# Two tokens a partition for V, tiles of 32 keys, and a first weight slice cast by two engines

## The chip, the cores and the metric

The kernel runs on one core of a Trainium2 chip. Five engines work side by side on it: TensorE (PE in the profile; PEld is its weight load), VectorE (DVE), ScalarE (ACT), GpSimd (POOL) and SyncE (SP), which here issues nearly all transfers (SPq in the profile). The metric is the time of one execution on the device, in microseconds (us); less is better. The kernel before takes 278.19 us, the median of three runs (277.95 to 278.23).

## The reference: what is computed

Attention inside chunks of 64 tokens (8 batches, 8 heads, 576 tokens, 64 numbers a head), and behind it a two-layer network with a squared ReLU on all 4608 tokens:

```
scores = scale * matmul(q_c, k_c^T)          # in chunks of 64 tokens
attn   = exp(scores - max) / (sum + 1e-9)
x      = matmul(attn, v_c)                    # [4608, 512], heads side by side
h      = max(x @ w_in, 0)                     # w_in  [512, 2048]
out    = (h * h) @ w_out                      # w_out [2048, 512]
```

Inputs and output are float32. The kernel multiplies in bfloat16 and leaves the maximum out of the exponential, which does not change the quotient.

## The kernel before, in words

The tokens are cut into 18 groups of 256, and two groups make a block of 512 tokens, so there are nine blocks. For each block the network's first layer runs 16 feature tiles of 128 (`ffn_in`, L621 for its matmuls), the second runs after it (`ffn_out_by_ft` for block 0, L795; `ffn_out` for the others, L678). The attention of the next blocks is set by hand into slots between these matmuls (L392, L420 and others), and the loads for later blocks go out on SP in between. The order within each engine is the program's own: nothing is rearranged by a planner, and an instruction that waits holds back all behind it on its engine.

The change lies in the start, where the attention of block 0 has no earlier work to hide behind. It is done by heads, not by tokens: half 0 is heads 0 to 3 of the block's 512 tokens, half 1 is heads 4 to 7. In the order of the program:

- `load_half` (L235) loads Q and K of each half, 512 KB each, with four tokens a partition, in pieces of 1024 bytes. SP issues Q0, K0, Q1, K1 (L238).
- `load_v_half` (L244) loads V, for each half in four transfers of 128 KB, one for each 128 tokens; a partition holds one token, so pieces have 256 bytes (L247). V goes into memory that the array `w_sum` needs only later, with a column of ones beside each head (memset at L231), so that the values product gives the sum of the exponentials too.
- `load_w_in(0, n_cast=2)` (L837): SP issues the first of eight slices of w_in, 512 KB for 256 features (L173), into one of five staging buffers `w_st`; POOL casts it to bfloat16 in two pieces of 128 features (L176).
- `transpose_half` (L255) transposes Q and K on PE and copies the result out of PSUM (L277, DVE and ACT). `scores_half` (L279) makes the scores of a half, keys on the partitions, as 32 matmuls of 64 keys by 64 queries (L289), and ACT takes the exponential (L296).
- `values_half` (L301) multiplies for half u and tokens 256j to 256j + 255: 16 matmuls of 64 by 65 (L309), a reciprocal (L316) and a product (L317) on DVE. `transpose_x_half` (L323) turns the result for the network (L325 on PE, copied by ACT or DVE at L329).
- `keep_busy(n)` (L333) issues n matmuls on constants, whose result nobody reads (L337).

Scores and values use two PSUM buffers in turn (`ps_att`), the rest four (`ps_ffn`). Two feature tiles of the network are begun (`begun`) before `ffn_in` takes over: they use the half of the input that comes from heads 0 to 3 first.

After the start SP issues the other seven slices of w_in and eight of w_out (L181), each cast on POOL, and with them Q, K and V of group 2, then of group 3 (L110, L158, L162). A staging buffer is free for slice i + 5 when the cast of slice i is done.

Of the kernel before, what the change touches and what calls it, by code (L numbers as in the profile page):

```python
# [10 lines left out]
FP32 = mybir.dt.float32  # L11
BF16 = mybir.dt.bfloat16
AF = mybir.ActivationFunctionType
ALU = mybir.AluOpType
# [3 lines left out]
def kernel(  # L18
# [9 lines left out]
    nc = tc.nc  # L28

    B, H, S, D = q.shape  # L30
# [4 lines left out]
    n_hp = H // 2  # L35
# [131 lines left out]
        for f in pieces:  # L167
            f()

    def load_w_in(i, n_cast=1):  # L170
        cols = slice(i * 256, (i + 1) * 256)
        st = wst_pool.tile([128, 1024], FP32, name="w_st").rearrange("p (a f) -> p a f", a=n_dt)
        nc.sync.dma_start(out=st, in_=moe_w_in[:, cols].rearrange("(a p) f -> p a f", p=128))  # L173
        n = 256 // n_cast
        for c in range(0, 256, n):
            nc.gpsimd.tensor_copy(  # L176
                out=w_in_bf[:, :, i * 256 + c:i * 256 + c + n], in_=st[:, :, c:c + n])
# [34 lines left out]
    def transpose_qk(g, q_pool, k_pool):  # L212
# [13 lines left out]
            transpose_paired(g, which, bank)  # L226
            copy_paired(copy, qkT[:, which], bank)

    v_first = w_sum.rearrange("p i f c -> p (i f c)")[:, 0:8 * H * (D + 1)].bitcast(
        FP32).rearrange("p (t h d) -> p t h d", t=4, h=H)  # L230
    nc.gpsimd.memset(v_first[:, :, :, D:D + 1], 1.0)  # L231

    first = chunks[blocks[0][0]][0]
# [9 lines left out]

    def load_v_half(u):  # L244
        b, s = first
        for t in range(4):
            nc.sync.dma_start(  # L247
                out=v_first[:, t, 4 * u:4 * u + 4, 0:D],
                in_=v[b, 4 * u:4 * u + 4, s + 128 * t:s + 128 * t + 128, :].rearrange(
                    "h s d -> s h d"))  # L250

# [27 lines left out]
    def scores_half(qkT):  # L279
# [3 lines left out]
        for h in range(2):  # L283
# [17 lines left out]
    def values_half(e, x, u, j):  # L301
        v_bf = v_first.bitcast(BF16)
        ps = ps_att.tile([128, 2, 512], FP32, name="ps_att")
        for t in range(2):
            for h in range(2):
                for a in range(2):
                    for p in range(2):
                        o0 = (2 * t + h) * (D + 1)
                        nc.tensor.matmul(  # L309
                            out=ps[64 * p:64 * p + 64, a, o0:o0 + D + 1],  # L310
                            lhsT=e[64 * p:64 * p + 64, a, h, 2 * j + t, :],
                            rhs=v_bf[64 * p:64 * p + 64, 2 * j + t, 4 * u + 2 * h + a, 1::2],
                            start=True, stop=True)
        o = ps[:, :, 0:4 * (D + 1)].rearrange("p a (h d) -> p a h d", d=D + 1)
        rec = att_pool.tile([128, 2, n_hp], FP32, name="rec", bufs=4)
# [688 lines left out]
```

## Time and profile before

| | |
|---|---|
| median of three runs | 278.19 us (277.95 to 278.23) |
| profiled execution, its time | 277.18 us |
| its span in the trace | 275.4 us |
| granted TensorE clock | 1.00 |
| PE busy | 267.3 us, 97% |
| first matmul of the network (L621) | 17.89 us |
| first matmul of block 0's second layer (L795) | 32.02 us |
| transposes of K of group 3 (L201) | 49.20 us |

All times inside an execution come from the one profiled execution and count from the start of its span. The time of that execution is 1.8 us longer than its span, and 1.0 us shorter than the median of the runs without a profile. A row of the timeline gives start, busy time, engine, line, operation, what is written and what is read, and in brackets how long the engine had been idle and what ended it. In the windows each row is a stretch of time, followed by the busy time of PE, PEld, DVE, ACT and POOL with their counts, the granted clock, the mean busy share of the 16 DMA engines and the rate in GB/s.

### The profile page before, as it was taken

The page shows a single profiled execution, that of the slowest core. Times are in us where ns is not written, and L with a number is a line of the kernel's source. Part 1 is how long each engine was busy: PE and PEld are TensorE (multiplying, and loading weights), DVE is VectorE, ACT ScalarE, POOL GpSimd, SP SyncE. Part 2 cuts the span into 40 slices and gives each one's busy share as a digit, 9 for nine tenths or more (in the row PEclk, how much of TensorE's full clock was granted, in tenths as well). Part 3 has the DMA queues.
Part 4 walks back from the last instruction along what each step waited for, and adds up shares of the span by engine and source line. Part 5 has one row for each costly group of instructions (what it writes and reads, how often), then busy time and mean ns, then how long its engine had stood idle before and what let it go on. Part 6 is the DMA issues. An engine that isn't in the chain of part 4 may idle for free.

```text
span 275.4 us, 7355 instructions
## 1 busy us (share of the span) xinstructions
PE 267.3 (97%) x3047; PEld 185.5 (67%) x3047; DVE 202.2 (73%) x313; ACT 155.5 (56%) x262; POOL 92.9 (34%) x106
## 2 busy tenths in 40 slices
PE   7889999999999999999999999999999999999994
PEld 4544454888775587658755875587658755875683
DVE  1546516689986997599769776977599769777793
ACT  1537605796347782768186918682768186317710
POOL 2037768140433800380029002900380029003412
PEclk9999999999999999999999999999999999999999
DMA  7999999999999999999999799858799981623004
GB/s 233 228 334 356 369 340 233 227 224 181 286 167 189 261 199 176 292 236 185 259 249 210 153 187 286 189 115 181 225 280 181 210 317 38 193 47 108 0 2 152
DMA packets 136417, 57.11 MB, mean 207 GB/s; under 512 B 110336, under 2 KB 130048, under 8 KB 136384
## 3 DMA queue, kind: packets, MB, share of 16 engines
q1 hardware_dynamic: 135968, 55.72, 86.8%
q0 software_dynamic: 272, 0.79, 0.7%
q8 instruction: 24, 0.39, 0.6%
q10 hardware_dynamic: 144, 0.13, 0.1%
q14 instruction: 9, 0.07, 0.1%
HBM read 36.70 MB, written 9.44 MB: 168 GB/s over the span
## 4 chain that ended last, share of the span: by engine, by line
PE 81%; DMA 9%; SPq 7%; POOL 1%; issue 1%; DVE 0%
PE ps_ffn L678 36%; PE ps_ffn L621 32%; PE ps_ffn L508 8%; DMA w_st<-in_moe_w_in_dram 5%; SPq L247 3%; PE ps_att L420 2%; DMA k_sb<-in_k_dram 2%; DMA w_st<-in_moe_w_out_dram 2%; PE ps_att L392 2%; SPq L162 1%; POOL w_in_bf L176 1%; SPq L158 1%; SPq L238 1%; PE ps_att L447 1%; SPq L181 0%
## 5 line engine op out<-in xcount | busy, mean ns | idle before, releaser
L621 PE MATMUL ps_ffn<-xT,w_in_bf 128*128 128x512 bf16 (+1 forms) x528 | 111.2, 353 | 0.4 <-POOL w_in_bf L176 0.4
L634 POOL TENSOR_TENSOR gT<-rl 128x512 bf16<-128x512 f32 x40 | 45.9, 1162 | 121.1 <-ACT rl L585 120.2
L621 PEld LDWEIGHTS <-w_in_bf 128*128 128x128 bf16 x528 | 50.6, 98 | 37.2 <-POOL w_in_bf L176 1.8
L678 PEld LDWEIGHTS <-w_st 128*128 128x128 bf16 x640 | 62.2, 98 | 7.3
L585 ACT ACTIVATE rl<-ps_ffn 128x512 f32<-128x512 f32 x84 | 50.1, 597 | 29.3 <-PE ps_ffn L621 29.0
L634 DVE TENSOR_TENSOR w_st<-gT 128x2048 bf16<-128x2048 bf16 x40 | 47.4, 1219 | 6.0 <-ACT gT L588 5.9
L678 PE MATMUL ps_ffn<-w_out_bf,w_st 128*128 128x256 bf16 x384 | 45.1, 273 | 0.0
L634 DVE TENSOR_TENSOR gT<-rl 128x512 bf16<-128x512 f32 x30 | 20.8, 693 | 22.6 <-ACT rl L585 22.2
L678 PE MATMUL ps_ffn<-w_sum,w_st 128*128 128x256 bf16 x256 | 29.6, 273 | 0.0
L678 PEld LDWEIGHTS <-gT 128*128 128x128 bf16 x256 | 24.7, 98 | 5.1 <-ACT gT L588 0.6
L612 ACT ACTIVATE rl<-ps_ffn 128x256 bf16<-128x256 f32 (+1 forms) x48 | 20.4, 455 | 6.6 <-PE ps_ffn L621 5.6
L525 DVE SCALAR_TENSOR_TENSOR gT<-rl 128x512 bf16<-128x512 f32 x21 | 23.2, 1103 | 0.4
L616 DVE TENSOR_TENSOR gT<-rl 128x256 bf16<-128x256 bf16 (+1 forms) x41 | 16.2, 438 | 9.6 <-ACT rl L612 9.5
L785 ACT COPY o_sb<-ps_ffn 128x512 f32<-128x512 f32 x7 | 4.1, 587 | 33.6 <-PE ps_ffn L678 33.6
L428 DVE TENSOR_TENSOR x<-ps_att,rec 128x512 bf16<-128x512 f32 x32 | 22.1, 692 | 1.1
L403 ACT ACTIVATE e<-ps_att 128x1024 bf16<-128x1024 f32 x16 | 15.8, 1025 | 4.8 <-PE ps_att L392 4.8
L508 PEld LDWEIGHTS <-w_dif 128*128 128x128 bf16 x140 | 12.9, 98 | 7.1
L678 PE MATMUL ps_ffn<-w_out_bf,gT 128*128 128x256 bf16 x128 | 15.6, 273 | 0.0
L678 PE MATMUL ps_ffn<-w_sum,gT 128*128 128x256 bf16 x128 | 15.3, 273 | 0.0
L176 POOL CAST w_in_bf<-w_st 128x1024 bf16<-128x1024 f32 (+1 forms) x9 | 8.9, 1000 | 17.9 <-DMA w_st<-in_moe_w_in_dram 17.9
L795 PE MATMUL ps_ffn<-w_out_bf,gT 128*128 128x512 bf16 x64 | 14.5, 380 | 0.0
L588 ACT ACTIVATE gT<-rl 128x512 bf16<-128x512 f32 x21 | 13.3, 632 | 0.7
(81 smaller groups left out, 288.8 us busy)
## 6 DMA issues: line engine op xcount, KB each, us to landing
q_sb<-in_q_dram SPq DMA_DIRECT2D x16, 512.0 KB, 6.2
out_dram<-o_sb SPq DMA_DIRECT2D x14, 512.0 KB, 4.6
k_sb<-in_k_dram SPq DMA_DIRECT2D x24, 256.0 KB, 5.9
w_st<-in_moe_w_in_dram SPq DMA_DIRECT2D x8, 512.0 KB, 6.7
w_st<-in_moe_w_out_dram SPq DMA_DIRECT2D x8, 512.0 KB, 6.1
ve_sb<-in_v_dram SPq DMA_DIRECT2D x28, 128.0 KB, 3.7
vo_sb<-in_v_dram SPq DMA_DIRECT2D x21, 128.0 KB, 3.3
k_sb<-in_k_dram SPq DMA_DIRECT2D x4, 512.0 KB, 6.8
```

Source lines behind the costliest of these rows:

```text
L403: nc.scalar.activation(out=e_out, in_=s_in, func=AF.Exp, scale=scale)
L428: nc.vector.tensor_tensor(out=x[:, t].rearrange("p h a d -> p a h d"), in0=o[:, :, :, 0:D], in1=rec.to_broadcast([128, 2, n_hp, D]), op=AL ...
L508: nc.tensor.matmul(out=out[:, 256 * f:256 * f + 256], lhsT=a[:, d, 128 * f:128 * f + 128], rhs=b[:, :, d, :], start=(first and f == 0 and ...
L525: later.append(lambda: nc.vector.scalar_tensor_tensor(out=place_of(i, jj), in0=both(x), scalar=0.0, in1=both(x), op0=ALU.max, op1=ALU.mult))
L585: nc.scalar.activation(out=rl, in_=h, func=AF.Relu)
L588: nc.scalar.activation(out=gT[:, ft], in_=rl, func=AF.Square)
L612: nc.scalar.activation(out=rl[:, 0:n], in_=h[:, 0:n], func=AF.Relu)
L616: nc.vector.tensor_tensor(out=gT[:, ft, c:c + n], in0=rl[:, 0:n], in1=rl[:, 0:n], op=ALU.mult)
L621: nc.tensor.matmul(out=h[:, 0:n], lhsT=w_in_bf[:, dt, ft * 128:(ft + 1) * 128], rhs=xT[:, c // 128:(c + n) // 128, dt, :], start=(dt == 0) ...
L634: engine.tensor_tensor(out=out, in0=in0, in1=in1, op=op)
L678: nc.tensor.matmul(out=outs[t], lhsT=a[:, i, t * 128:(t + 1) * 128], rhs=b[:, i, :], start=(first and i == 0 and (last or t == 0)), stop=( ...
L795: nc.tensor.matmul(out=o_ps[tt], lhsT=gT[:, ft, tt * 128:(tt + 1) * 128], rhs=w_out_bf[:, ft, :], start=(ft == 0), stop=(ft == n_ft - 1))
```

## The change

V of heads 0 to 3 is laid out anew: a partition holds two neighbouring tokens, so two transfers of 256 KB in pieces of 512 bytes take the place of four of 128 KB in pieces of 256 bytes. V of heads 4 to 7 stays as it was. Since the 64 keys of a chunk then lie on 32 partitions, even and odd keys apart, the scores of half 0 are made in tiles of 32 keys (64 matmuls instead of 32) and the values as two products of 32 keys that add up in PSUM (32 matmuls instead of 16). The column of ones stands ahead of the even token and behind the odd one, so that the two sums land in different columns; a reduction on DVE adds them before the reciprocal.

The first w_in slice is loaded at the same place in SP's order, but its cast is taken out of `load_w_in` and put behind the last transposes, as four pieces of 2 x 128 features by 128: POOL casts those of feature tile 0, ACT those of feature tile 1. Slices 1 to 3 are cast in two pieces each, no longer in one. In the order of PE, `values_half(e1, 1)` moves ahead of the transposes of x(1,0), and the two `keep_busy` calls of 4 and 6 become 2 and 3.

```diff
-    def load_w_in(i, n_cast=1):
+    def load_w_in(i, n_cast=1, cast=True):
...
+        if not cast:
+            return st
...
+    VE = 2 * D + 2
+    HH = H // 2
+    v_first = w_sum.rearrange("p i f c -> p (i f c)").bitcast(FP32)
+    v_pairs = v_first[:, 0:2 * HH * VE].rearrange("p (t h e) -> p t h e", t=2, h=HH)
...
+    nc.gpsimd.memset(v_pairs[:, :, :, 0::VE - 1], 1.0)
...
     def load_v_half(u):
         b, s = first
+        if u == 0:
+            for t in range(2):
+                nc.sync.dma_start(
+                    out=v_pairs[:, t, :, 1:1 + 2 * D],
+                    in_=v[b, 0:4, s + 256 * t:s + 256 * t + 256, :].rearrange(
+                        "h (s i) d -> s h (i d)", i=2))
+            return
...
+    def scores_pairs(ps, qT, kT):
+        for h in range(2):
+            for t in range(2):
+                for i in range(2):
+                    for c in range(4):
+                        for a in range(2):
+                            rows = slice(64 * a, 64 * a + 64)
+                            o0 = a * 512 + h * 256 + t * 128 + i * 64
+                            nc.tensor.matmul(
+                                out=ps[32 * c:32 * c + 32, o0:o0 + 64],
+                                lhsT=kT[rows, h, 4 * t + c, i::2],
+                                rhs=qT[rows, h, 4 * t + c],
+                                start=True, stop=True, tile_position=(64 * a, 32 * c))
+
+    def values_pairs(e, x, j):
...
+        for h in range(2):
+            for a in range(2):
+                for i in range(2):
+                    for c in range(4):
+                        t, p = divmod(c, 2)
+                        rows = slice(32 * c, 32 * c + 32)
+                        o0 = (2 * h + a) * (D + 2) + i
+                        nc.tensor.matmul(
+                            out=ps[64 * p:64 * p + 64, t, o0:o0 + n],
+                            lhsT=e[rows, a, h, 2 * j + i, :],
+                            rhs=v_bf[rows, j, 2 * h + a, 1::2][:, i * n:i * n + n],
+                            start=(h == a == i == 0), stop=(i == 1),
+                            skip_group_check=True, tile_position=(32 * c, 64 * p))
...
+        nc.vector.tensor_reduce(
+            out=rec, in_=o[:, :, :, 0::D + 1], op=ALU.add, axis=mybir.AxisListType.X)
+        nc.vector.reciprocal(out=rec, in_=rec)
+        nc.vector.tensor_tensor(
...
-    load_w_in(0, n_cast=2)
+    w_first = load_w_in(0, cast=False)
...
-    e0 = scores_half(qkTs[0])
+    e0 = scores_half(qkTs[0], pairs=True)
...
-    values_half(e0, xs[0], 0, 0)
+    values_pairs(e0, xs[0], 0)
     keep_busy(2)
     e1 = scores_half(qkTs[1])
-    values_half(e0, xs[0], 0, 1)
+    values_pairs(e0, xs[0], 1)
     transpose_x_half(xs[0], 0, 0, A, bank_bf16())
-    keep_busy(4)
-    values_half(e1, xs[1], 1, 0)
+    keep_busy(2)
+    values_half(e1, xs[1], 0)
     transpose_x_half(xs[0], 0, 1, A, bank_bf16())
-    keep_busy(6)
+    values_half(e1, xs[1], 1)
+    keep_busy(3)
     xb = [bank_bf16(), bank_bf16()]
     begun = {ft: ps_ffn.tile([128, 512], FP32, name="ps_ffn") for ft in range(2)}
     transpose_x_half(xs[1], 1, 0, A, xb[0])
-    values_half(e1, xs[1], 1, 1)
     keep_busy(3, begun[0])
     transpose_x_half(xs[1], 1, 1, V, xb[1])
+    for dt in (slice(0, 2), slice(2, 4)):
+        for ft, copy in enumerate((nc.gpsimd.tensor_copy, nc.scalar.copy)):
+            cols = slice(128 * ft, 128 * ft + 128)
+            copy(out=w_in_bf[:, dt, cols], in_=w_first[:, dt, cols])
...
     for i in range(1, 8):
-        load_w_in(i)
+        load_w_in(i, n_cast=2 if i < 4 else 1)
```

More of the change, by code (lines that the diff above doesn't have):

```diff
@@ L227, in transpose_qk @@
             copy_paired(copy, qkT[:, which], bank)
-    v_first = w_sum.rearrange("p i f c -> p (i f c)")[:, 0:8 * H * (D + 1)].bitcast(
-        FP32).rearrange("p (t h d) -> p t h d", t=4, h=H)
+    VE = 2 * D + 2
+    HH = H // 2
+    v_first = w_sum.rearrange("p i f c -> p (i f c)").bitcast(FP32)
+    v_pairs = v_first[:, 0:2 * HH * VE].rearrange("p (t h e) -> p t h e", t=2, h=HH)
+    v_first = v_first[:, 2 * HH * VE:2 * HH * VE + 4 * HH * (D + 1)].rearrange(
+        "p (t h d) -> p t h d", t=4, h=HH)
+    nc.gpsimd.memset(v_pairs[:, :, :, 0::VE - 1], 1.0)
     nc.gpsimd.memset(v_first[:, :, :, D:D + 1], 1.0)
@@ L245, in load_v_half @@
         b, s = first
+        if u == 0:
[5 more added lines that the diff above has]
+            return
         for t in range(4):
             nc.sync.dma_start(
-                out=v_first[:, t, 4 * u:4 * u + 4, 0:D],
+                out=v_first[:, t, :, 0:D],
                 in_=v[b, 4 * u:4 * u + 4, s + 128 * t:s + 128 * t + 128, :].rearrange(
@@ L277, in transpose_half, with scores_half @@
             copy(out=out_, in_=in_)
-    def scores_half(qkT):
+    def scores_pairs(ps, qT, kT):
[12 more added lines that the diff above has]
+    def values_pairs(e, x, j):
+        v_bf = v_pairs.bitcast(BF16)
+        ps = ps_att.tile([128, 2, 512], FP32, name="ps_att")
+        n = D + 1
+        for h in range(2):
[11 more added lines that the diff above has]
+                            skip_group_check=True, tile_position=(32 * c, 64 * p))
+        o = ps[:, :, 0:4 * (D + 2)].rearrange("p t (b d) -> p t b d", d=D + 2)
+        rec = att_pool.tile([128, 2, n_hp], FP32, name="rec", bufs=4)
+        nc.vector.tensor_reduce(
+            out=rec, in_=o[:, :, :, 0::D + 1], op=ALU.add, axis=mybir.AxisListType.X)
+        nc.vector.reciprocal(out=rec, in_=rec)
+        nc.vector.tensor_tensor(
+            out=x[:, 4 * j:4 * j + 4].rearrange("p (t b) a d -> p t (b a) d", t=2),
+            in0=o[:, :, :, 1:1 + D],
+            in1=rec.to_broadcast([128, 2, n_hp, D]),
+            op=ALU.mult)
+    def scores_half(qkT, pairs=False):
         qT, kT = (qkT[:, w].rearrange("c t h q -> c (t h q)").rearrange(
@@ L282, in scores_half @@
         ps = ps_att.tile([128, 1024], FP32, name="ps_att")
-        for h in range(2):
+        if pairs:
+            scores_pairs(ps, qT, kT)
+        for h in range(0 if pairs else 2):
             for t in range(4):
@@ L299, in scores_half, with values_half @@
         return flat.rearrange("p (a h t q) -> p a h t q", a=2, h=2, t=4)
-    def values_half(e, x, u, j):
+    def values_half(e, x, j):
         v_bf = v_first.bitcast(BF16)
@@ L311, in values_half @@
                             lhsT=e[64 * p:64 * p + 64, a, h, 2 * j + t, :],
-                            rhs=v_bf[64 * p:64 * p + 64, 2 * j + t, 4 * u + 2 * h + a, 1::2],
+                            rhs=v_bf[64 * p:64 * p + 64, 2 * j + t, 2 * h + a, 1::2],
                             start=True, stop=True)
```

## The prediction

> **What bounds the kernel now.** I read the page first.
>
> ```profile
> PE 267.3 (97%) x3047; PEld 185.5 (67%) x3047; DVE 202.2 (73%) x313; ACT 155.5 (56%) x262; POOL 92.9 (34%) x106
> ...
> PE 81%; DMA 9%; SPq 7%; POOL 1%; issue 1%; DVE 0%
> ```
>
> PE is nearly always busy; what is not PE on the chain lies in the first 50 us. So I read the chain of waits there, in two windows (start, duration, what):
>
> ```profile
> 10.12 1.56 SPq L247
> ...
> 12.28 0.51 SPq L173
> 12.79 0.04 issue
> 12.83 5.73 DMA w_st<-in_moe_w_in_dram
> ...
> 42.96 6.20 DMA k_sb<-in_k_dram
> 49.15 0.04 issue
> 49.20 0.64 PE ps_ffn L201 x16
> ```
>
> One string of transfers runs from the V issues (L247) over w_in (L173) and w_out to the K of group 3, which lands at 49.15 and is taken up by PE at 49.20. Behind that PE is the chain to the end. A gain must therefore move two things: the moment from which PE runs without a break, and this string. The first is in the timeline (start, duration, engine, instruction, idle time before and its cause):
>
> ```profile
> 17.07 0.40 PE L325 MATMUL ps_ffn<-ident,x 128*128 128x128 bf16 x4 [0.60 <-DVE x L317]
> 17.22 1.17 POOL L176 CAST w_in_bf<-w_st 128x512 bf16<-128x512 f32 x2 [14.94 <-DMA w_st<-in_moe_w_in_dram]
> 17.51 0.42 DVE L329 COPY xT<-ps_ffn 128x512 bf16<-128x512 bf16 x1 [0.49 <-PE ps_ffn L325]
> ...
> 17.89 2.46 PE L621 MATMUL ps_ffn<-xT,w_in_bf 128*128 128x512 bf16 x10 [0.41 <-POOL w_in_bf L176]
> 18.44 0.98 PEld L621 LDWEIGHTS <-w_in_bf 128*128 128x128 bf16 x6 [0.44 <-POOL w_in_bf L176]
> ```
>
> Two paths meet at 17.89: w_in slice 0 (landed about 17.17, then a cast) and the attention of the first block, whose last transposes start at 17.07. From there PE has no listed idle time up to 80 us. The transfers by windows (the last two numbers are the share of the 16 DMA engines and GB/s):
>
> ```profile
> 10.50:11.00 0.50, 0.32 (x10) 0.21 (x11) 0.45 (x1) 0.50 (x1) 0.00 (x0) 1.00 1.08 192
> ...
> 11.50:12.00 0.50, 0.50 (x34) 0.33 (x32) 0.47 (x2) 0.00 (x0) 0.00 (x0) 1.00 0.65 118
> 12.00:12.50 0.50, 0.18 (x10) 0.17 (x9) 0.28 (x1) 0.43 (x1) 0.00 (x0) 1.00 0.24 49
> ...
> 46.00:46.50 0.50, 0.50 (x34) 0.33 (x22) 0.47 (x3) 0.49 (x1) 0.50 (x1) 1.00 1.04 305
> ```
>
> V in pieces of 256 bytes moves at about 190 GB/s with full queues; Q and K of group 3, mostly in pieces of 512 bytes, at 305. Between them stands a hole: at 11.5 to 12.5 the DMA engines are half empty, because the seventh V issue (10.12, 1.56 us) was held up.
>
> **The change part by part.**
>
> *V of heads 0 to 3.* Four issues of 128 KB in 256-byte pieces become two of 256 KB in 512-byte pieces. 524 KB take 2.76 us at 190 GB/s and 1.73 us at 305: 1.03 us less in front of w_in. Bounds: 0 if a 512-byte piece costs as much as two small ones; 1.7 if the two issues removed from SP also close the hole, which holds 0.35 x 0.5 + 0.76 x 0.5 = 0.55 us. The w_in issue would stand in the held seventh place, but with all of V already issued ahead of it, so the hole may be covered; I take 0.2 of the 0.55, nearer zero because the hold may return in another place. The string moves by 1.2 us. The loads are the first on their way, so nothing hides this. [...]
>
> *First w_in slice.* Before: two POOL casts of 128x512 (0.61 each), PE starting 0.67 after the first began and its second column tile waiting 0.44 more. After: four pieces of 128x256, two on POOL and two on ACT beside them. No such POOL piece is in the trace; 128x128 takes 0.29 and 128x512 0.61, so 0.29 to 0.61, and I take 0.40. ACT copies 128x256 in 0.37 (L783). PE can start 0.21 sooner after the landing, and the 0.44 goes. ACT now waits for the slice with only the relus queued behind it (first at 19.52), which need PE's result anyway. Slices 1 to 3 are cast in halves: 1.22 instead of 1.04 on POOL, against 1.5 between the casts now (20.55, 22.06, 23.57), hidden; their first half is ready 0.43 sooner, which pays the waits of 0.29 and 0.49 that the weight loads show at 19.71 and 21.64. The later buffer release, 0.18, is covered by four transfers already queued.
>
> *Scores of the first half.* 64 matmuls instead of 32. Same streamed columns over more tiles, so no less than the 0.50 of L289 if all eight run together; at L289's spacing, (0.50 - 0.20)/31 = 10 ns, 64 take 0.83. I take that: 0.33 more. Hidden: PE's next hard point is the second K, landed at 9.73; exp moves from 9.39 to 9.72 at its end and is needed at 10.46. Without that cover it would cost 0.33.
>
> *Values of the first half, twice.* 32 matmuls of 32 rows instead of 16 of 64. L420 runs 32 of 65 columns in 0.46 as one group (45.80 to 46.26); L309's two-tile form, 16 in 0.45, would give 32 x 17 ns + 0.19 = 0.73. I take 0.46. DVE gains a reduction over pairs; the nearest row is the reciprocal 128x8 at 0.21, plus 0.03 between: 0.24 each. They lie on the chain values, normalise, transpose.
>
> *Order and fillers.* keep_busy falls from 4 and 6 (plus an unchanged 3) to 2 and 3: five fewer matmuls of 0.11 (three take 0.50, one of them alone 0.28), 0.55 us in PE's order. values(e1, second) moves ahead of the transposes of x(1,0), so its reciprocal and product (0.21 + 0.69) follow those of the half before. Walked through: second K in PE at 9.80 to 10.44; values(e0,0) 10.46 to 10.95 (its V lands with the first pair, no later than before); DVE product done 12.2; scores(e1) 11.3, exp done 12.85; values(e0,1) 12.25 to 12.7, product done 13.9; values(e1,0) 13.4; transposes 13.95; values(e1,1) 14.35, needing the last V (14.83 before, about 13.7 now); products done 14.83 and 15.8; last transposes 15.83 to 16.2. Against 17.47 that is 1.3 sooner. With the dear value of each doubt (0.27 twice on values) it is 16.75.
>
> *Small.* One more POOL memset, 0.1 us at 2.3, before SP is free at 2.84.
>
> *Sum.* Slice 0 lands at 17.17 - 1.2 = 15.97; plus 0.05, 0.40 and 0.06 PE starts at 16.5, behind the transposes at 16.2: 1.4 sooner. PE then needs K of group 3 at 49.20 - 1.4 = 47.8 and it lands at 49.15 - 1.2 = 47.95: a wait of about 0.2 is late next. So 1.2 us remain, and run on to the end since PE is the chain. Profiled: span 275.4 to 274.2, its time 277.18 to 275.98. The median of the runs is 278.19, 1.0 above the profiled one; less 1.2: **277.0**.
>
> **The rivals.**
>
> *The transfer gains nothing (B).* Pieces of 512 bytes cost twice, or SP's hold, not the packets, paces the string. For it: the hold of 1.56 with DMA idle. Against: share over 1 at 10 to 11. PE then starts 0.2 sooner by the cast, but K of group 3 stays at 49.15 and PE waits for it: 0 to 0.1 gained, 278.1.
>
> *The attention is the bound (D).* The 32-row matmuls don't overlap: 32 x 28 ns (65 columns at the pace of 0.11 for 256) + 0.17 = 1.07, 0.6 more twice. The last transposes end at 16.2 + 1.2 = 17.4 or a little later and PE starts at 17.6, but with all slices there: 64 matmuls take 64 x 0.216 = 13.8 instead of the 14.1 from 17.89 to 32.02. 0.3 and 0.3, with something off for the reduction: 0.5 gained, 277.7. Against: L420 overlaps four tiles.
>
> *PE falls to half pace (C), slower.* At the start 12 fillers take 2.74 (228 ns each), later six take 0.82 (137 at most). With five fewer fillers and a late slice 0 the FFN could begin at the early pace. It decides if PE's share in 13 to 17 falls clearly below the 4.50 of 6 us that it now has at 12 to 18. At start the slow pace lasted from 1.72 to about 6; four such us lose 2.0 and nothing hides it: starting 1.4 sooner PE is 0.6 behind, 278.8. Against: my walk keeps PE busy 80% of 12.2 to 16.2, with one gap of 0.3. [...]
>
> **How the numbers follow.** Forecast 0.65: 276.4 (hole closed, K early) to 277.6. B 0.08, D 0.10, C 0.17, into which I put losses of a like size that the profile does not show. No change means within 0.2%, 0.56 us, about what a measurement of this kernel can tell. The forecast gives faster 0.63 and same 0.02, B same 0.08, D lies at the line and gives faster 0.04 and same 0.06, C slower: faster 0.67, same 0.16, slower 0.17. The range runs from the forecast's low end over D and B to 278.2, leaving out C and a little below.
>
> **What would show it.** Right: two V issues of 256 KB landing by 11.5, SP at w_in by 11.7, first w_in cast near 16, L621 from 16.5, K of group 3 near 48. Wrong, each by its sign: w_in landing at 17 with V at 190 GB/s (B); last L325 after 17 with value groups of 1 us (D); the first L621 matmuls over 400 ns apart (C); or PE idle for over 0.5 at 47 to 50, the gain given back there.

## The result, and the profile after

The changed kernel takes 278.94 us, the median of 20 runs (277.96 to 281.18), and the kernel before takes 277.69 (276.61 to 279.97, 20 runs). The ratio is 1.0051, with a 95% interval of 1.0030 to 1.0071: slower by half a per cent, where 277.0 had been forecast. The profiled execution of the changed kernel took 278.93 us, with a span of 277.2 against 275.4 before. All ratios, and the medians given with them, leave out executions in a slower state of the chip: five of twelve in the kernel with 64 early rows, one each in two others.

The page of the changed kernel, parts 1 to 4:

```profile
PE 267.7 (97%) x3103; PEld 186.3 (67%) x3106; DVE 203.5 (73%) x315; ACT 155.9 (56%) x264; POOL 93.1 (34%) x110
...
PEclk9979999999999999999999999999999999999999
...
q8 instruction: 24, 0.39, 0.6%
...
PE 91%; DMA 4%; DVE 2%; issue 1%; ACT 0%
```

PE is as busy as before and holds more of the chain (91% against 81%). The transfers of w_in and w_out have left the chain; that of K of group 3 is still on it, as the next view shows. One thing is new: a slice of the granted clock, at 14 to 21 us, reads 7. Another was there before too and now matters: `q8 instruction`, by its name the queue that brings the engines' programs, moved 24 pieces of 16 KB each. PE's program before has 6094 matmuls and weight loads (3047 of each on the page); if each is a row of the program and most pieces are PE's, one holds some 250 rows, an estimate from 6094 and 24.

The chain of waits of the changed kernel (start, duration, what):

```profile
12.53 0.26 PE ps_att L318 x8
12.78 2.03 issue
14.81 0.39 PE ps_att L318 x24
...
44.36 6.01 DMA k_sb<-in_k_dram
50.37 0.04 issue
50.41 0.64 PE ps_ffn L203 x16
```

In the middle of the second value group of heads 0 to 3, between its eighth and ninth matmul, PE stands for 2.03 us and waits for nothing that the profile shows ("issue"). K of group 3 is taken up at 50.41, 1.21 later than before.

By windows (PE, PEld, DVE, ACT and POOL busy; then granted clock, DMA share, GB/s):

```profile
13.00:14.00 1.00, 0.00 (x0) 0.00 (x0) 0.00 (x0) 0.07 (x1) 0.00 (x0) 1.00 1.01 311
14.00:15.00 1.00, 0.19 (x21) 0.19 (x23) 0.00 (x0) 0.00 (x0) 0.00 (x0) 1.00 1.10 356
15.00:16.00 1.00, 1.00 (x37) 0.63 (x27) 0.68 (x3) 0.43 (x1) 0.00 (x0) 0.75 1.09 366
16.00:17.00 1.00, 1.00 (x22) 0.67 (x18) 0.86 (x3) 0.15 (x1) 0.06 (x1) 0.50 1.11 353
...
18.00:19.00 1.00, 1.00 (x9) 0.86 (x8) 0.61 (x1) 0.15 (x1) 0.59 (x2) 0.54 1.07 351
...
20.00:22.00 2.00, 2.00 (x11) 0.92 (x10) 0.50 (x1) 1.13 (x3) 1.81 (x4) 1.00 0.79 253
```

After the stop the granted clock is 0.50 for 3.4 us, from about 15.5 to 18.9: the rows of 0.75 and 0.54 are stretches that hold both paces. Once PE is at full clock again, at 20 to 24, the transfers have a hole: 253 and 252 GB/s, where the kernel before moved 359 and 348 (same view of the kernel before):

```profile
20.00:22.00 2.00, 2.00 (x10) 0.77 (x9) 1.79 (x3) 1.53 (x4) 1.04 (x1) 1.00 1.10 359
22.00:24.00 2.00, 2.00 (x11) 0.88 (x9) 0.62 (x2) 1.81 (x4) 1.47 (x2) 1.00 1.10 348
```

The timeline of the changed kernel, where before stood the cast and the first matmuls of the network:

```profile
16.95 0.74 POOL L928 CAST w_in_bf<-w_st 128x256 bf16<-128x256 f32 x2 [14.65 <-DMA w_st<-in_moe_w_in_dram]
19.31 1.96 PE L679 MATMUL ps_ffn<-xT,w_in_bf 128*128 128x512 bf16 x8
19.60 0.37 SPq L173 DMA_DIRECT2D w_st<-in_moe_w_in_dram  x1
```

The slice lands for 16.95 (before 17.22; in this execution Q0, the first transfer of all, came 0.64 later than before), PE reaches the network only at 19.31 instead of 17.89, and SP issues its sixth w_in slice at 19.60 instead of 18.42 (timeline of the kernel before):

```profile
18.42 3.57 SPq L173 DMA_DIRECT2D w_st<-in_moe_w_in_dram  x3
```

### The profile page after: what moved, and what is told of

Read it like the earlier page. It is cut to its first block, busy times and chain, and to the rows that moved or that the text cites. A ratio compares the mean times of both kernels' runs of the same rounds, so it can differ in the third digit from the quotient of the medians.

```text
span 277.2 us, 7471 instructions
## 1 busy us (share of the span) xinstructions
PE 267.7 (97%) x3103; PEld 186.3 (67%) x3106; DVE 203.5 (73%) x315; ACT 155.9 (56%) x264; POOL 93.1 (34%) x110
## 4 chain that ended last, share of the span: by engine, by line
PE 91%; DMA 4%; DVE 2%; issue 1%; ACT 0%
PE ps_ffn L736 36%; PE ps_ffn L679 35%; PE ps_ffn L566 8%; PE ps_ffn L853 4%; PE ps_att L478 2%; DMA k_sb<-in_k_dram 2%; PE ps_att L450 2%; DMA q_sb<-in_q_dram 2%; PE ps_ffn L395 1%; PE ps_ffn L282 1%; PE ps_ffn L383 1%; DVE gT L674 1%; DVE x L486 1%; DVE qkT L291 0%; PE ps_att L505 0%
## 5 line engine op out<-in xcount | busy, mean ns | idle before, releaser
L674 DVE TENSOR_TENSOR gT<-rl 128x256 bf16<-128x256 bf16 (+1 forms) x41 | 17.1, 465 | 9.6 <-ACT rl L670 9.5
L670 ACT ACTIVATE rl<-ps_ffn 128x256 bf16<-128x256 f32 (+1 forms) x48 | 20.3, 453 | 4.0 <-PE ps_ffn L679 3.4
L692 DVE TENSOR_TENSOR w_st<-xT 128x1024 bf16<-128x1024 bf16 (+1 forms) x21 | 12.2, 635 | 0.8 <-ACT xT L510 0.8
```

What stands on the lines that cost most here:

```text
L670: nc.scalar.activation(out=rl[:, 0:n], in_=h[:, 0:n], func=AF.Relu)
L674: nc.vector.tensor_tensor(out=gT[:, ft, c:c + n], in0=rl[:, 0:n], in1=rl[:, 0:n], op=ALU.mult)
L692: engine.tensor_tensor(out=out, in0=in0, in1=in1, op=op)
```

## The experiments

Each edit is told against the kernel named. Ratios are to the kernel before on the same chip; its medians were 278.00, 277.91, 277.84, 277.62 and 277.66 in the five groups of runs.

**First group: what is the stop?** Theory I: the pairs put 64 more matmuls and as many weight loads into PE's program ahead of the values, so that PE reaches the end of the piece it holds before the next one is usable. Its rivals were that the 32-row matmuls themselves, or the double issue of work at this place, stop PE.

Kernel before, with the score and value matmuls of heads 0 to 3 issued twice (the same number of extra instructions, no pairs):

```diff
+                        for _ in range(times):
...
-    e0 = scores_half(qkTs[0])
+    e0 = scores_half(qkTs[0], times=2)
...
-    values_half(e0, xs[0], 0, 0)
+    values_half(e0, xs[0], 0, 0, times=2)
```

> The kernel before, but each score and value matmul of the first half is issued twice, with the same operands and result. V, casts, order and fillers are those of before. PE's program then has as many instructions up to the second value group as in the changed kernel. Theory I (instruction supply: PE stops after its instruction 445, counted in its program, until the next piece of the program has come by the instruction queue): PE pauses with no visible cause, 'issue', for 1 to 3 us in the second value group of the first half, in front of its ninth matmul, and the time is 0.5 to 2.5 us above before. Rival II (the pause is a hidden wait of the new V layout or of its 32-row matmuls): no pause, time within 0.3 us of before.

278.27 us, ratio 1.0007 [0.9979, 1.0035], and no stop: a miss for Theory I in this form. In its profile the piece of program began to move at 10.1 us and PE reached the place at about 12.7; in the eight profiles with a stop PE went on 2.6 to 2.8 us after the piece had begun to move, so here, by that figure, PE came to the place at about the moment when it needed no wait.

Changed kernel, with 64 more rows in the first filler group:

```diff
-    keep_busy(12)
+    ps0 = ps_ffn.tile([128, 512], FP32, name="ps_ffn")
+    keep_busy(5, ps0)
+    for _ in range(39):
+        nc.tensor.matmul(out=ps0[0:32, 0:32], lhsT=ident[:, 0:32], rhs=ident[:, 0:32], start=True, stop=True)
```

> The changed kernel, but the first filler group is 5 matmuls of 256 columns and 39 of 32 columns in place of 12 of 256: about as long, while PE waits for the first Q anyway, with 64 more PE instructions. Theory I: the pause stays at instruction 445 and so moves to other work: it stands in the scores of the second half, in front of their ninth matmul, from about 11.7 to 14 or later; none in the value groups. Time as the changed kernel, within 1 us. Rival II: the pause stays in the second value group, in front of the ninth matmul.

279.03 us, ratio 1.0045 [1.0006, 1.0084]. The stop moves by as many rows as were put in front, out of the values into the scores before them (its profiled execution took 285.3 us, so only the place is read):

```profile
13.16 0.38 PE L347 MATMUL ps_att<-qkT 64*64 64x64 bf16 x23 [1.47 <-issue]
```

So the stop belongs to a place in the program, not to an instruction: in both kernels row 446 of PE's program, counted from 0, is the last that runs before it.

Changed kernel without the pairs (V, scores and values as before; order, fillers and casts as changed):

```diff
-    e0 = scores_half(qkTs[0], pairs=True)
+    e0 = scores_half(qkTs[0])
...
-    values_pairs(e0, xs[0], 0)
+    values_half(e0, xs[0], 0, 0)
```

> The changed kernel without the pairs: V, scores and values as before, with the new casts, order and fillers. Instruction 445 is then the last but one matmul of the last value group, at about 14.5 us, as late after instruction 190 as 5.9 us. Theory I: a pause of at most 0.5 us, PE warm, network from 17.4 to 17.8; its K of group 3 lands as before, so 0 to 0.5 us faster than before. Rival III (order and fillers cost the time, since PE falls to half pace when it has fewer fillers): granted clock 0.5 in a stretch before 18 us and 0.5 to 1.5 us slower than before.

279.07 us, ratio 1.0035 [1.0001, 1.0069]. No stop, full clock, and slower all the same, though only just clear of noise. Its profile doesn't show the loss: that execution took 277.26, the fastest of the twelve. The stop is not likely to be the whole cause.

Kernel before with the pairs alone (order, fillers and casts as before):

```diff
-    w_first = load_w_in(0, cast=False)
+    load_w_in(0, n_cast=2)
...
-    keep_busy(2)
+    keep_busy(4)
     values_half(e1, xs[1], 0)
...
-        load_w_in(i, n_cast=2 if i < 4 else 1)
+        load_w_in(i)
```

(against the changed kernel; the second filler group and the order of `values_half(e1, 1)` go back likewise)

> The kernel before with the pairs alone: V of heads 0 to 3 with two tokens a partition, its scores in tiles of 32 keys, its values in two products; casts, order and fillers as before. Theory I: the pause of about 2 us is there, in front of the ninth matmul of the second value group, clock 0.5 behind it, and the time is 0.5 to 2.5 us above before, about that of the changed kernel. Rival III: no half pace, time at or below before.

278.64 us (275.91 to 279.47), ratio 1.0010 [0.9976, 1.0044], with the stop, but a shorter one than expected, and with the full clock behind it in the profile:

```profile
13.05 0.39 PE L318 MATMUL ps_att<-w_sum,e 32*64 32x65 bf16 x24 [0.44 <-issue]
```

In the eight profiles with a stop at this row, here and below, it ended 2.6 to 2.8 us after a piece of program began to move: 10.2 and stop over at 13.05 here, 12.0 and 14.81 in the changed kernel. Over all twenty profiles the piece came anywhere between 10.0 and 12.0 us.

**Second group: stop, or transfers?** Theory IV took the hole in the transfers: the cast by two engines holds up a staging buffer.

The changed kernel once more, without an edit:

> The changed kernel once more, beside the next three on the same chip. Theory I (PE stops after its instruction 445 until the next piece of its program can be used, 2.8 us after that piece shows in the instruction queue; if it stands idle for long, it falls to half pace): a stop again in front of the ninth matmul of the second value group; its end is the piece's row in the instruction queue plus 2.8 us; the granted clock below 0.995 in most of the runs; 0.3 to 0.7% slower than before. Rival V (the one traced run was unlucky): no stop above 0.5 us, clock full in most runs, time within 0.2% of before.

278.95 us, ratio 1.0030 [1.0012, 1.0048]; a stop of 0.64 and full clock afterwards. PE reaches the network at 16.96, 0.93 sooner than before, and yet K of group 3 is taken up at 50.28, after a wait. The half pace is absent from this profile, which shows what else is wrong.

Changed kernel, with slice 0 cast by POOL at its load as before:

```diff
-    w_first = load_w_in(0, cast=False)
+    load_w_in(0, n_cast=2)
...
-    for dt in (slice(0, 2), slice(2, 4)):
-        for ft, copy in enumerate((nc.gpsimd.tensor_copy, nc.scalar.copy)):
```

> The changed kernel with the first w_in slice cast as before, by POOL alone and as soon as it lands. Rival IV (ACT's share of the cast stands behind the attention's last copies, frees the staging buffer late, and so leaves a hole in the transfers): no hole at 16 to 22 us, K of group 3 0.3 to 1 us earlier, time 0.3 to 1 us below the changed kernel. Theory I: stop and half pace as in the changed kernel, time within 0.3 us of it.

277.96 us (276.46 to 279.58), ratio 0.9991 [0.9962, 1.0019]: 1.0 us better, though its profiled execution has a stop of 1.54 and the half clock from 13.5 to 20.3 us. K of group 3 comes no earlier there (50.53), against what was expected. Slices 1 to 3 are still cast in halves here, so this is not the cause. In the timeline of the changed kernel's second profile, the cast of slice 1 and SP's sixth w_in issue, and then two of its windows:

```profile
17.45 1.17 POOL L178 CAST w_in_bf<-w_st 128x512 bf16<-128x512 f32 x2 [0.67 <-DMA w_st<-in_moe_w_in_dram]
18.65 0.37 SPq L173 DMA_DIRECT2D w_st<-in_moe_w_in_dram  x1
```

```profile
22.00:24.00 2.00, 2.00 (x11) 0.94 (x10) 0.53 (x2) 1.19 (x2) 1.78 (x3) 1.00 0.75 241
24.00:30.00 6.00, 6.00 (x30) 2.70 (x29) 3.62 (x7) 4.68 (x8) 3.91 (x4) 1.00 0.99 294
```

The same views of the kernel with POOL's cast, with the cast of slice 0 and the same issue:

```profile
16.29 1.17 POOL L178 CAST w_in_bf<-w_st 128x512 bf16<-128x512 f32 x2 [14.00 <-DMA w_st<-in_moe_w_in_dram]
17.49 0.37 SPq L173 DMA_DIRECT2D w_st<-in_moe_w_in_dram  x1
```

```profile
22.00:24.00 2.00, 2.00 (x11) 0.93 (x10) 1.82 (x3) 1.52 (x3) 1.29 (x2) 1.00 1.10 351
24.00:30.00 6.00, 6.00 (x30) 2.71 (x28) 3.97 (x6) 4.64 (x9) 5.05 (x5) 1.00 1.05 376
```

With POOL's cast the sixth issue follows the end of slice 0's cast (16.29 + 1.17 = 17.46). In the changed kernel it follows the end of slice 1's (17.45 + 1.17 = 18.62). SP's program says the same: the changed kernel's sixth slice waits for the transfer and cast of slice 1, the seventh for slice 2's, the eighth for slice 3's, the first w_out for slice 4's, and only the second w_out takes slice 0's buffer, on a wait for ScalarE. Before, the sixth slice waits for slice 0's cast, and so on. So of five staging buffers one stays empty from the casts of slice 0 to the tenth transfer, and the sixth to ninth issues each come one cast later than they could. In these stretches 241 and 294 GB/s are moved instead of 351 and 376.

Changed kernel with six matmuls of 512 columns ahead of the second value group, so that PE comes to row 446 later:

```diff
+    ps_hold = ps_ffn.tile([128, 512], FP32, name="ps_ffn")
-    keep_busy(2)
+    keep_busy(2, ps_hold)
     e1 = scores_half(qkTs[1])
+    for _ in range(6):
+        nc.tensor.matmul(out=ps_hold, lhsT=ident, rhs=kh[1][:, 0:2, :, 1::2], start=True, stop=True)
     values_pairs(e0, xs[0], 1)
```

> The changed kernel with six matmuls of 512 columns that nobody reads between the scores of the second half and the second value group: 1.3 us of PE time, in which the next piece of the program comes in. Theory I: PE comes to instruction 445 at 13.3 or later, the stop shrinks to 0 to 1 us, PE has worked meanwhile and stays at full pace: clock at or above 0.998 in more than half of the runs, and the time 0.2 to 1.0 us below the changed kernel in spite of 1.3 us more work. Rival VI (the loss is a plain lengthening of the attention): 0.5 to 1.3 us slower than the changed kernel.

278.88 us, ratio 1.0033 [1.0008, 1.0059]. No stop, no half pace in the profile, and nothing won that could be told from noise: with the buffer lost, PE waits 0.96 for K of group 3, which it takes up at 51.40.

The pairs alone, with the same six matmuls:

> The pairs alone (casts, order and fillers as before) with the same six matmuls of 512 columns ahead of the second value group. Theory I: stop at most 1 us, full clock in more than half of the runs where the pairs alone had it in 4 of 12, and 0 to 0.8 us below the pairs alone, so at or below before. Rival VI: 0.5 to 1.3 us slower than the pairs alone.

277.26 us (276.31 to 278.96), ratio 0.9975 [0.9953, 0.9998], 11 of 12 executions at full clock. (Full clock means here a mean granted clock of 0.999 or more; one stretch of 3.4 us at half pace brings the mean to 0.994.)

**Third group: is it the buffer, or the cast on ScalarE?** The changed kernel with slice 0 loaded into space of its own (that of `w_dif`, written first by `w_difference(0)`); the two-engine cast stays:

```diff
-    w_first = load_w_in(0, cast=False)
+    w_first = w_dif[:, 0:4].rearrange("p i f c -> p (i f c)").bitcast(FP32).rearrange(
+        "p (a f) -> p a f", a=n_dt)
+    nc.sync.dma_start(out=w_first, in_=moe_w_in[:, 0:256].rearrange("(a p) f -> p a f", p=128))
```

> The changed kernel as it is, two-engine cast and all, except that the first w_in slice is loaded into a buffer of its own (the space of w_dif, unused until w_difference(0)) instead of one of the five staging buffers, so that none of the five is held by a tile that two engines release. Theory IV (what costs about 1.0 us in the changed kernel is the one staging buffer that stays out of the rotation until the tenth transfer, and not the cast on two engines): SP issues its seventh w_in slice without waiting for any cast, bytes moved between 20 and 26 us stay at 340 GB/s or more (the changed kernel's second run: 241 at 22 to 24), PE no longer waits 0.8 us for a w_in cast nor 1.1 us for K of group 3; the median is 0.8 to 1.5 us under the changed kernel's 278.9, that is 277.4 to 278.1, with the program stop of Theory I still there in front of row 446 (0.4 to 2 us). Rival (the cast on ACT itself, or the n_cast=2 of slices 1 to 3, costs the time): 278.6 to 279.2 as before, with the transfers at full rate.

277.15 us (276.22 to 278.66), ratio 0.9970 [0.9944, 0.9995], 1.8 us under the changed kernel: a little more than expected, and not found to this extent again (fifth group). Its profile has a stop of 0.32 and the half clock from about 12.6 to 19.5, and six slices go out without waiting for a cast, not seven as expected; the transfers are whole again (windows):

```profile
22.00:24.00 2.00, 2.00 (x11) 0.88 (x10) 0.82 (x2) 1.70 (x4) 1.70 (x2) 1.00 1.10 349
24.00:30.00 6.00, 6.00 (x30) 2.73 (x28) 4.59 (x6) 4.64 (x9) 4.40 (x5) 1.00 1.07 376
```

Kernel before with the cast part of the change alone:

```diff
-    load_w_in(0, n_cast=2)
+    w_first = load_w_in(0, cast=False)
...
+    for dt in (slice(0, 2), slice(2, 4)):
+        for ft, copy in enumerate((nc.gpsimd.tensor_copy, nc.scalar.copy)):
...
-        load_w_in(i)
+        load_w_in(i, n_cast=2 if i < 4 else 1)
```

> The kernel before with the cast part of the change alone: slice 0 loaded without a cast, its four pieces cast by POOL and ScalarE after the last x transposes, slices 1 to 3 in two column halves; V, scores, values and fillers as before. Its program's staging buffers turn round a little differently from the changed kernel's: SP's sixth and seventh w_in slices wait for slice 1's and slice 2's casts instead of slice 0's and 1's, and only the eighth takes slice 0's buffer, so that two issues are one cast late and not four. Theory IV: the sixth issue at about 19.6 and the seventh at about 20.8 (before: 18.4 and the next cast's end), a hole of some 0.6 to 1.2 us in the transfers between 20 and 24 us, slower than before by 0.2 to 1.0 us (278.1 to 278.9 against 277.9), no stop of PE in its program. Rival (the cast part is worth 0.2 to 0.4 us, as the prediction's step took it, and the buffer costs nothing): 277.5 to 277.7.

278.65 us, ratio 1.0028 [1.0005, 1.0052]: slower by 0.8 us, without pairs and without a stop. The sixth issue came at 20.20, after slice 1's cast (19.00 + 1.17), the seventh at 23.00, and PE waits for a cast (timeline):

```profile
19.00 1.17 POOL L178 CAST w_in_bf<-w_st 128x512 bf16<-128x512 f32 x2 [0.71 <-DMA w_st<-in_moe_w_in_dram]
...
22.48 10.54 PE L623 MATMUL ps_ffn<-xT,w_in_bf 128*128 128x512 bf16 x48 [0.81 <-POOL w_in_bf L178]
```

In every kernel with the lost buffer the cast of slice 0 is given in part to a second engine and also stands late in the program, behind the last transposes. No run separates the two. Two programs that were built from the changed kernel, but not run, do: with all four pieces on POOL at the late place, and with the pieces on POOL and ACT right behind the load, SP's sixth slice waits for slice 0's casts again. So by the programs it takes both, a piece on a second engine and a late place for it.

The other two took both causes away: the first has the edit of POOL's cast, the second that of the staging apart, and both that of the six matmuls:

> The changed kernel with both suspected causes taken away: slice 0 cast by POOL at its load, as before, and six matmuls of 512 columns between the second half's scores and the second value group of the first, so that PE reaches row 446 of its program after its next piece is there. Theory I with Theory IV (both costs are real and add up): no stop with no releaser in the first 20 us, granted clock 0.9 or more in 13 to 20 us, no hole in the transfers; 276.9 to 277.5, 0.5 to 1.0 us under the kernel before and 0.4 to 1.0 us under the run with the cast by POOL alone (277.96). Rival (the six matmuls cost on the path what the stop cost): 277.9 to 278.3.

> As the run with the staging of its own (two-engine cast kept), and with the six matmuls of 512 columns as well. Theory I with Theory IV: no program stop, no hole, a sixth staging buffer in effect; 276.6 to 277.4, at or up to 0.4 us under the run with POOL's cast and the six matmuls, since the cast on two engines then gives what the prediction took for it (PE can start 0.2 us sooner) and the next casts on POOL begin 0.5 us sooner. If the two-engine cast itself costs the time: 0.5 us or more above that run.

277.30 us, ratio 0.9984 [0.9957, 1.0010], and 277.61, ratio 0.9977 [0.9948, 1.0007]. The first is as expected; the second is 0.2 above what was expected and not better than without the six matmuls: beside the staging apart, the stop's cost can't be seen in the median.

**Fourth group: a sixth buffer, and the price of the stop.** With slice 0 apart, five buffers remain for the rest. The kernel before with only that:

```diff
-    load_w_in(0, n_cast=2)
+    w_first = w_dif[:, 0:4].rearrange("p i f c -> p (i f c)").bitcast(FP32).rearrange(
...
+    for c in range(0, 256, 128):
+        nc.gpsimd.tensor_copy(out=w_in_bf[:, :, c:c + 128], in_=w_first[:, :, c:c + 128])
```

> The kernel before, with slice 0 loaded into the space of w_dif, so that all five staging buffers serve the slices behind it; nothing else is changed. If the transfers of 18 to 50 us are bound by the rate of the DMA engines (350 to 370 GB/s there already) a sixth buffer gives nothing: 277.6 to 278.0, K of group 3 at 49.2 as before, and the 0.7 us of the changed kernel with its own staging are V's. If the buffers bound them: 277.0 to 277.4, and most of those 0.7 us are the sixth buffer's.

277.57 us, ratio 0.9999 [0.9985, 1.0013]. A sixth buffer is worth nothing that this run could show; losing the fifth costs.

The pairs alone, without and with the six matmuls, on one chip, and with the staging apart:

> The kernel before with the pairs alone (V of heads 0 to 3, scores and values in tiles of 32 keys; cast, order and fillers as before), beside its partner with the six matmuls on one chip. Theory I (the stop and the half pace behind it cost as much as V's shorter transfer gains): a stop of 0.4 to 2 us in front of row 446, granted clock below 0.9 in part of 13 to 20 us in half of the executions, median 277.8 to 278.7 against 277.9 for the kernel before. Rival (the stop is covered and V gives what was taken for it): 276.7 to 277.3.

> The same with six matmuls of 512 columns between the second half's scores and the second value group. Theory I: no stop, full clock in nearly all executions, 276.9 to 277.5, at least 0.6 us under the run without the six matmuls. Rival (the stop costs nothing in the median, and the six matmuls nothing either): within 0.4 us of the run without them.

> The pairs alone, with slice 0 in the space of w_dif, cast by POOL as before. Theory (the sixth buffer gives nothing of itself): within 0.4 us of the pairs alone, stop and half pace included. If the sixth buffer gives the gain: 0.5 to 0.8 us under the pairs alone, as far as the kernel before with its own staging is under the kernel before.

278.47 us (ratio 1.0021 [0.9997, 1.0045]), 277.59 (1.0000 [0.9979, 1.0020]) and 278.32 (1.0012 [0.9985, 1.0040]). The six matmuls save 0.9 here. But the profile with them still has a stop, of 0.54, the one without shows full clock behind its stop of 0.48, and the gain over the kernel before that the six matmuls had shown in the second group (0.9975) was not found again. So 0.9 is their worth in this group, and by which way is not shown. The third is within 0.4 us of the pairs alone, as expected if a sixth buffer gives nothing; but its profile has the half clock without any stop (window):

```profile
13.00:14.00 1.00, 1.00 (x29) 0.86 (x18) 0.59 (x3) 0.14 (x1) 0.00 (x0) 0.50 1.05 326
```

Among its executions the three at full clock took 276.88 us in the mean, the four with a mean clock under 0.9915 took 279.44; in the first run of the pairs alone four took 277.12 and three 279.37. In these two runs, then, executions with more half pace are longer. But PE needs no stop to fall into it: here it had only been kept waiting for K, V and DVE (0.62, 0.36 and 0.54) between 9 and 12.4 us.

**Fifth group: V, or cast and order?** The changed kernel with its own staging again, and the same without the pairs:

> The changed kernel with slice 0 in a space of its own, beside its partner without the pairs. Held to the earlier run of it: 276.7 to 277.6, ratio under 1; executions at full clock near 276.6, those with a mean clock of 0.99 or less 0.7 to 1.5 us above them, since only those go through the half pace behind the stop.

> The changed kernel without the pairs (V, scores and values as before), with its two-engine cast, order and fillers, and slice 0 in a space of its own. If the rest of the gain is that of V's shorter transfer: 277.4 to 278.0, w_in's first cast at 16.7 or later, no stop, full clock. If it is that of cast, order and fillers: 276.7 to 277.2, at or under the partner with the pairs; then V's gain and the pairs' stop cancel.

277.61 us (276.63 to 279.31), ratio 1.0005 [0.9980, 1.0030], and 278.09, ratio 1.0007 [0.9980, 1.0035]. The first had been 0.9970; its advantage over the kernel before was not found again either, and the clock did not sort its executions this time (six at full clock 277.77, three lowest 278.14). The same kernel at 0.9970 and at 1.0005 also says how far a single ratio can be trusted. What did hold is that without the buffer loss it is level with the kernel before or a little better, and that cast, order and fillers by themselves bring nothing.

All ratios by what the kernel has:

| kernels | ratios | mean |
|---|---|---|
| slice 0 in the ring, cast late by two engines (six runs, the changed kernel twice) | 1.0028 to 1.0051 | 1.0037 |
| pairs, buffer whole, no matmuls in front of row 446 (six runs) | 0.9970 to 1.0021 | 1.0002 |
| pairs, buffer whole, six matmuls there (four runs) | 0.9975 to 1.0000 | 0.9984 |
| no pairs, buffer whole (three runs) | 0.9999 to 1.0007 | 1.0004 |

No run with the lost buffer is under 1.0028 and none without the loss is over 1.0021. The loss is worth 0.35%, 1.0 us (first row less second). By the programs of the two kernels without the pairs, only two issues come late and not four; their ratios, 1.0035 and 1.0028, are little lower. No version beats the kernel before beyond doubt; the third row comes nearest, with 0.16% in the mean. What the six matmuls take away, in most profiles the stop and the half pace, is worth about half a us by the second and third row, but single pairs of kernels with and without them lie anywhere from 0.5 dearer to 1.4 cheaper, so this price stays open. V's shorter transfer is then worth 0.2%, some 0.5 us, by the third and fourth, an estimate of the same weakness.

## Why the prediction was wrong

The forecast took 1.2 us off the time and the change added 1.25 to it. Point by point:

- **First w_in slice, the step that failed.** "The later buffer release, 0.18, is covered by four transfers already queued" priced the release by its duration. What counted is which buffer the next transfer is given: with a second engine reading slice 0's late in the program, SP's program gives it slice 1's, and one of five stays empty while four issues come one cast late. That costs 1.0 us, shown both ways: taking it away gives 277.96, 277.15 and 277.61 instead of 278.94 and 278.95, putting the cast part alone into the kernel before gives +0.8. The rest of the step held in its sizes: two pieces took 0.74 on POOL, where 0.80 was taken.
- **Scores and Values twice: a term that was missing.** Their times were right or dear: 64 score matmuls took 0.61 to 0.68 on PE (0.83 was taken), a value group 0.46, the reduction 0.17. But the 64 extra matmuls came with as many weight loads, and in eight profiles PE stood for 0.3 to 2.0 us at one row of its program, until 2.6 to 2.8 us after a piece of 16 KB had begun to move. This is in no term of the sum. The run with 64 more rows shows that the place is fixed by the program; how much the stop costs on average is open.
- **V of heads 0 to 3: right.** (The upper bound of 1.7 is by its own terms 1.03 + 0.55 = 1.6; nothing hangs on it.) SP is at w_in by 10.45 to 11.56, by 10.65 in the changed kernel (before 12.28; 11.7 had been named). The first cast starts at 15.98 in the median of the 14 profiles with the new V and at 17.39 in that of the six with the old: 1.4 sooner, where 1.2 was taken. Rival B, by which nothing is gained here, is out.
- **Order and fillers: right, but for the stop.** In the second profile of the changed kernel PE reaches the network at 16.96 (16.5 was summed), in spite of a stop of 0.64. Rival D, the attention as the bound, is out.
- **Sum: only half arrives.** K of group 3 was to be taken up at 47.95, from 49.20 before. With the old V and all buffers it was taken up at 49.20 to 51.10 in four profiles, 50.0 in the mean, so the one profile that the sum started from was the earliest of them. With the pairs and all buffers the mean of ten is 49.5: 0.5 sooner, not 1.2. It was 48.41 to 49.62 in seven of the ten. In one it was 50.53, behind half pace; in two, 50.16 and 50.98, PE waited for it (0.9 and 1.1). In those two the third w_in slice could be cast only at 21.1 and 21.2, though it had been issued at 12.5 and 13.0; among the profiles with the new V its cast starts anywhere between 19.0 and 21.2, and why was not found. So a string that starts 1.4 sooner did not end 1.4 sooner.
- **Rival C gave 278.8, and its mechanism is there, but it does not set the time.** The granted clock did fall to 0.50, in the changed kernel and in four more profiles, in the changed one behind the stop. But with the six matmuls, eight of twelve executions at full clock and a profile without half pace, the changed kernel still takes 278.88, and with its own staging it takes 277.15 with the half clock in the profile (277.61, run again). That 278.8 comes so near to 278.94 is chance. The larger loss was among those that C's chance was to cover and no rival named.
- **The base was high as well:** the median of three, 278.19, against 277.69 in 20 runs.

## What to carry to other kernels

Before a second engine is given part of a cast, look at who releases the staging buffer, how late in its program, and which transfer is next to take it, in the order that the issuing engine's program has; the buffer that dropped out of a ring of five cost 1.0 us here, where cast, order and fillers by themselves brought nothing. When a change adds many small matmuls near the start, count PE's instructions and not only their time: here the queue `q8 instruction` moved 24 pieces of 16 KB, and PE stood for up to 2.03 us at one row of its program. And a gain of 0.3% that one run of 12 executions shows is not yet a gain: two kernels here showed it once and lost it in the next group.

## What the runs showed of the hardware

- **PE stood at one row of its program.** In eight profiles it stood there for 0.3 to 2.0 us, with nothing in the waits but "issue", and went on 2.6 to 2.8 us after a piece of 16 KB had begun to move, at 10.2 to 12.0 us. That PE had run out of program is the reading that fits these figures and the run with 64 more rows; no view names it. Why the piece comes at 10.0 in one profile and 12.0 in another, with the data queues full (DMA share 1.25 at 8 to 12 us in the changed kernel), stays open.
- **The half clock does not need a long idle stretch.** In the five profiles in which the granted clock falls to 0.50 before 20 us it stays there for 3.4 or 6.8 us. The falls come anywhere from 12.4 to 15.5 us. In the 3.41 us before the fall, as long as the half clock of the changed kernel lasts (15.50 to 18.91), PE had been busy for 0.94 us (changed kernel), 1.53 (POOL's cast), 1.79 (64 early rows), 1.89 (pairs with their own staging) and 1.96 (changed kernel with its own staging); in the profile with 1.89 no single wait was longer than 0.62. PE's busy time alone doesn't tell when the clock falls: in the second profile of the changed kernel PE was busy for 1.67 of the 3.00 us from 12 to 15, about the same share as 1.96 of 3.41, and the clock was 1.00 from there to 20 us. What decides was not shown.
- **Three DVE products took longer beside a cast on POOL.** Three products of 128 x 256 took 1.54 us in the changed kernel, with POOL casting beside them, and 0.84 in the kernel with the pairs alone, where POOL's cast was over before. The timelines of the one and of the other:

```profile
55.39 1.54 DVE L674 TENSOR_TENSOR gT<-rl 128x256 bf16<-128x256 bf16 x3 [1.74 <-ACT rl L670]
...
55.50 1.07 POOL L403 CAST qkb<-q_sb 128x1024 bf16<-128x1024 f32 x1 [5.85 <-DMA q_sb<-in_q_dram]
```

```profile
52.24 1.04 POOL L403 CAST qkb<-q_sb 128x1024 bf16<-128x1024 f32 x1 [5.30 <-DMA q_sb<-in_q_dram]
...
53.37 0.84 DVE L674 TENSOR_TENSOR gT<-rl 128x256 bf16<-128x256 bf16 x3 [1.49 <-ACT rl L670]
```

PE then waits 0.4 for x of group 3 (58.67 in the changed kernel's chain). Whether the two meet depends on when Q or K of a later group lands, so these 0.7 us of DVE and 0.4 of PE come and go with no edit at all: they are in seven of the profiles (1.46 to 1.65 us for the three products), that of the kernel before with its own staging among them, and not in the second profile of the changed kernel.
